# In the second layer's weight preparation, VectorE makes all low halves and GpSimd only the sums

## The chip, the cores and the metric

The kernel runs on one core of a Trainium2 chip. The time is the device time of one execution in microseconds (us), as the median of three timed runs. A profile of one further execution shows what each engine did: TensorE (PE in the rows, its weight loads PEld), VectorE (DVE), ScalarE (ACT), GpSimd (POOL) and SyncE (SP), which issues most DMAs.

## The reference

Attention with hash buckets gives `x` (1536 tokens x 512), and two dense layers follow. Only the second of them is touched here:

```
def _moe2_ref(x, w_in, w_out):        # x 1536x512, w_in 512x2048, w_out 2048x512
    h = x @ w_in
    g = h - np.tanh(h)
    return (g @ w_out).astype(np.float32)
```

The weights arrive as 64-bit words and are turned into 32-bit floats. A product in full precision is made of three TensorE products: each operand is split into a high half (the operand rounded to the format that TensorE multiplies fast) and a low half (the operand less its high half), and high*high, high*low and low*high are added up.

## The kernel before

After the attention and the first layer, `second_layer` works in two blocks (`sb` 0 and 1) of 768 tokens. Each block walks through 8 units `u`; a unit takes 256 of the 2048 hidden columns, so there are 16 units. In a unit, `h` is made by a scheme with seven instead of eight block products: the four blocks of the weights are combined into sums (`s1` to `s4`), the four blocks of the tokens into others (`t1` to `t4`, made once per block in `tokens`), and each of the seven products (`product`, L1084 to L1086, six matrix multiplications of 384 columns) goes into one of four PSUM banks. There are six PSUM slots `pt`; four of them hold results of the block through all units, so two are left for these banks, and TensorE can begin a further bank only when VectorE has read out an earlier one. These readings are `plus` (VectorE, `pl<-pt,ph` and `ph<-pt,ph` in the rows: bank plus an earlier partial sum) and, for one bank, `act`. In `act`, ScalarE makes `tanh` (L1097), VectorE subtracts (`pl<-pl,f` or `pl<-pt,f`), ScalarE rounds the result (L1099, `gh`), VectorE makes its low half (`gl<-pl,gh`). `outer2` (L1135) multiplies these by `w_out` and adds to the block's results.

`unit_weights` prepares a unit's weights. A DMA brings two tiles, `win` and `wout`, of 128 x 1024 floats. GpSimd makes four sums of 128x256 (`f<-wi`, `f<-f,wi`, `f<-wi,f`). Then four operand tiles and the two halves of `wout` are split: ScalarE writes the high half (L1056, L1061), another engine the low half by one subtraction. Before the change GpSimd makes four of these six low halves (all 128x512), and VectorE two (one 128x512, one 128x256). `tokens(1)`, the preparation of the second block's tokens, runs beside units of the first block, well ahead of use: GpSimd makes 16 sums and differences of 128x384 in the three buffers `t` (`t<-xh,xl`, `t<-t`), ScalarE rounds (L1002), VectorE makes eight low halves (`xl<-t,xh`, `t2l`, `t3l`, `t4l`).

All additions and subtractions go through one helper, so VectorE's and GpSimd's have one line, L890; the tiles in a row tell them apart. The order in which each engine gets its instructions is not the code's. Each operation is given to a planner (`op(engine, cost, key, ...)`) with a cost in us and a due time (`key`); `Plan.order` plays all engines forward by these costs and issues the operations in the order in which they start there. Every engine then works through its own list strictly in that order. The constants that this touches are `STEP = 1.06` (one product of a unit on TensorE) and the costs in `unit_weights`.

Of the kernel before, what the change touches and what calls it, by code (L numbers as in the profile page):

```python
# [123 lines left out]
class Plan:  # L124
# [11 lines left out]
    def buf(self, pool, tag, shape, dtype=F32):  # L136
        return Buf(self, pool, tag, shape, dtype)

    def op(self, eng, cost, key, fn, reads=(), writes=(), after=(), release=0.0, lat=None):
        o = Op()  # L140
        o.lat = self.LAT.get(eng, LATE) if lat is None else lat
        o.n, o.eng, o.cost, o.key, o.fn = len(self.ops), eng, cost, key, fn
        o.deps, o.users, o.bufs = {}, [], []
        for tok in reads:
            w = self.writer.get(tok)
            if w is not None:
                o.deps[w] = True
            self.readers.setdefault(tok, []).append(o)
        for tok in writes:
            w = self.writer.get(tok)  # L150
            if w is not None:
                o.deps[w] = True
            for r in self.readers.pop(tok, ()):
                if r is not o:
                    o.deps[r] = True
            self.writer[tok] = o
        for a in after:
            o.deps.setdefault(a, False)
        for tok in (*reads, *writes):
            b = tok[0] if isinstance(tok, tuple) else tok  # L160
            if isinstance(b, Buf) and b not in o.bufs:
                o.bufs.append(b)
                b.refs += 1
                self.by_pool.setdefault(b.pool, []).append(o)
        o.wait, o.ready = len(o.deps), release
        for d in o.deps:
            d.users.append(o)
        self.ops.append(o)
        return o
# [75 lines left out]
def tile_lsh_attention_moe(  # L245
# [13 lines left out]
    nc = tc.nc  # L259
# [18 lines left out]
    op, buf, room = plan.op, plan.buf, plan.room  # L278
# [65 lines left out]
    def dma(nbytes, key, out, in_, reads=(), writes=(), release=0.0):  # L344

        op("DMA", max(0.55, nbytes / 180e3), key, lambda: nc.sync.dma_start(out=out(), in_=in_()), reads, writes, release=release)
# [7 lines left out]
    def at(tick):  # L354
        return T_ATT + tick * TICK
# [324 lines left out]
    for g in range(len(pairs)):  # L680
# [7 lines left out]
        for n, (nm, half) in enumerate((("k", 0), ("q", 0), ("k", 1), ("q", 1))):  # L688
            key = k0 + PIECE * n * TICK if g else FIRST[n]
# [199 lines left out]
    def add(eng, out, in0, in1, sub=False):  # L889
        eng.tensor_tensor(out=out, in0=in0, in1=in1, op=ALU.subtract if sub else ALU.add)  # L890

    def unit_at(n):
        return moe_at(NBLK * KF) + n * UNIT
# [49 lines left out]
    def early(i, dtype=F32R):  # L943
        tag, pool = EARLY[i]
        return part2(pool, tag, dtype)
# [73 lines left out]
    def small(tag_pool):  # L1019
        pool, tag = tag_pool  # L1020
        return buf(pool, tag, [P, XB], F32)

    def unit_weights(sb, u):
        n = sb * NU + u
        odd = n % 2
        key = unit_at(n) - JIT - (UNIT0 if n < 2 else 0.0)
        gate = ["wd"] if odd else []
        w32 = [early(6 + 2 * odd + i, F32) for i in range(2)]
        for part in range(2):
            d = dram[u, part]  # L1030
            dma(
                P * DM * 8, unit_at(n) - FETCH + 3 * part, w32[part], lambda d=d: d.rearrange("p (m f) -> p m f", m=2),
                [("dram", u, part, i) for i in range(2)], [w32[part]], release=unit_at(n) - FETCH - 10.0,
            )
        win, wout = w32
        q = HB // 3 * 2

        def blk(i, j):
            return lambda: win()[:, i - 1, (j - 1) * q:j * q]

        sa, sb_ = (small(("f", "f")) for _ in range(2))
        lo_, up = slice(0, q), slice(q, 2 * q)
        op("POOL", 0.7, key, lambda: add(nc.gpsimd, sa()[:, up], blk(2, 1)(), blk(2, 2)()), [win], [(sa, 1)])
        op("POOL", 0.7, key + 0.1, lambda: add(nc.gpsimd, sa()[:, lo_], sa()[:, up], blk(1, 1)(), True), [win, (sa, 1)], [(sa, 0)])
        op("POOL", 0.7, key + 0.2, lambda: add(nc.gpsimd, sb_()[:, up], blk(1, 1)(), blk(2, 1)(), True), [win], [(sb_, 1)])
        op("POOL", 0.7, key + 0.3, lambda: add(nc.gpsimd, sb_()[:, lo_], blk(1, 2)(), sa()[:, lo_], True), [win, (sa, 0)], [(sb_, 0)])
        if odd:
            tiles = [buf("a2", f"a2{i}", [P, 2, DM], F32R) for i in range(4)]
        else:
            tiles = [early(10 + i) for i in range(4)]  # L1050
        srcs = (lambda: win()[:, 0], lambda: sa(), lambda: sb_(), lambda: win()[:, 1, q:])
        reads = ([win], [(sa, 0), (sa, 1)], [(sb_, 0), (sb_, 1)], [win])
        for i, (tl, src, rd) in enumerate(zip(tiles, srcs, reads)):
            w = DM if i < 3 else q
            eng, cost, e = (("POOL", 1.4, nc.gpsimd), ("DVE", 1.0, nc.vector))[i % 2]
            op("ACT", 0.02 + w * 0.00097, key + 0.5 + i, lambda tl=tl, src=src, w=w: nc.scalar.copy(tl()[:, 0, :w], src()), [*rd, *gate], [(tl, 0)], lat=0.4)  # L1056
            op(eng, cost * w / DM, key + 0.6 + i, lambda tl=tl, src=src, w=w, e=e: add(e, tl()[:, 1, :w], src(), tl()[:, 0, :w], True), [*rd, (tl, 0)], [(tl, 1)], lat=0.4)
        outs = []
        for i in range(2):
            tl = buf("raw", "raw", [P, 2, DM], F32R) if odd else early(14 + i)  # L1060
            op("ACT", 0.52, key + 5 + 2 * i, lambda tl=tl, i=i: nc.scalar.copy(tl()[:, 0], wout()[:, i]), [wout], [(tl, 0)], lat=0.4)  # L1061
            op("POOL", 1.4, key + 5.1 + 2 * i, lambda tl=tl, i=i: add(nc.gpsimd, tl()[:, 1], wout()[:, i], tl()[:, 0], True), [wout, (tl, 0)], [(tl, 1)], lat=0.4)
            outs.append(tl)
        at_ = {"a11": (0, 0), "a12": (0, q), "s2": (1, 0), "s1": (1, q), "s4": (2, 0), "s3": (2, q), "a22": (3, 0)}
        return {k: (tiles[i], o) for k, (i, o) in at_.items()}, outs
# [3 lines left out]
    def unit(sb, u, ops):  # L1069

        n = sb * NU + u
        key = unit_at(n)
        A, outs = unit_weights(sb, u)
        gs = [[buf("g2", x, [P, 2, HB], F32R) for x in ("gh", "gl")] for _ in range(2)]

# [103 lines left out]
    for m in range(KF):  # L1179
        for part, w in enumerate((w_in1, w_out1)):  # L1180
            if m < N_PRE:
                key = at(n_items - TICKS + C0) + (m + part / 2) * (TICKS - C0) * TICK / N_PRE
            else:
                key = T_MOE + (m - N_PRE + part / 2) * MTICK
# [85 lines left out]
```

## Time and profile before

| | us |
|---|---|
| median of three timed runs (775.41 to 777.13) | 775.73 |
| the profiled execution | 777.77 |
| its span, first to last instruction | 776.0 |
| second layer in it, about | 503 to 776 |
| block 1's tokens are prepared, about | 566 to 608 |
| first product of block 1, about | 638 |

The profiled execution is 2.04 us (0.26%) longer than the median; 1.77 us of it lie outside the span. In the second layer TensorE is the engine that hardly ever rests: from 500 to 776 us it stands still seven times, 7.3 us in all, before its last instruction.

### The profile page before, as it was taken

How to read it: one execution, taken by the hardware profiler on the slowest of the kernel's cores; microseconds unless marked ns; L12 is line 12 of the kernel's file. 1: busy time of each engine (PE TensorE's matmuls, PEld its weight loads, DVE VectorE, ACT ScalarE, POOL GpSimd, SP SyncE). 2: the span in 40 equal slices, each digit the busy share in tenths (PEclk: the TensorE clock that was granted, in tenths of full speed). 3: DMA queues.
4: the chain of work that ended last, by engine and by line, in shares of the span. 5: the costliest groups of instructions: out<-in, count | busy, mean ns of one | idle time of the engine just before them, and what ended most of it. 6: DMA issues, size and time to landing. Idle time of an engine off the chain costs nothing.

```text
span 776.0 us, 11414 instructions
## 1 busy us (share of the span) xinstructions
PE 755.0 (97%) x3901; PEld 655.8 (85%) x3901; DVE 562.5 (72%) x978; ACT 460.7 (59%) x926; POOL 400.8 (52%) x410
## 2 busy tenths in 40 slices
PE   7999999999999999999999999999998899999997
PEld 5999999999987888878887888888887798889885
DVE  6899899899998988754443566468689677667643
ACT  6999898998888556543333344365445355455422
POOL 5677668668545000022222386668599665656410
PEclk9999999999999999999999999999999999999999
DMA  6664656546690800035555417631111124111002
GB/s 171 166 154 117 139 131 141 138 106 145 164 394 3 344 37 0 28 95 174 165 160 166 146 58 225 210 115 62 56 55 54 55 67 175 58 55 57 26 1 82
DMA packets 32231, 91.05 MB, mean 117 GB/s; under 512 B 4518, under 2 KB 5414, under 8 KB 32172
## 3 DMA queue, kind: packets, MB, share of 16 engines
q1 hardware_dynamic: 31596, 89.69, 39.2%
q8 instruction: 31, 0.51, 0.3%
q10 hardware_dynamic: 576, 0.62, 0.2%
q14 instruction: 28, 0.23, 0.1%
HBM read 59.87 MB, written 11.53 MB: 92 GB/s over the span
## 4 chain that ended last, share of the span: by engine, by line
PE 82%; DVE 6%; ACT 3%; DMA 3%; POOL 2%; issue 2%; SPq 1%; ACTq 0%; POOLq 0%
PE pt L1135 10%; PE s L851 8%; PE pt L851 8%; PE pt L597 7%; PE pt L817 5%; PE pt L815 5%; PE pt L816 5%; PE s L1135 4%; PE pt L1084 4%; PE pt L1086 4%; PE pt L1085 4%; PE s L536 4%; PE s L537 4%; PE pt L575 4%; PE pt L576 4%
## 5 line engine op out<-in xcount | busy, mean ns | idle before, releaser
L932 POOL TENSOR_TENSOR t<-t,raw 128x512 uint32<-128x512 uint32 x32 | 45.1, 1409 | 163.0 <-ACT raw L927 114.0
L540 DVE TENSOR_SCALAR_CACHE_REDUCE p<-s 128x768 f32<-128x768 f32 x93 | 88.3, 950 | 14.5 <-PE s L537 13.7
L562 ACT ACTIVATE p<-p,mn 128x768 f32<-128x768 f32 x96 | 90.5, 943 | 10.2 <-DVE p L540 9.0
L597 PE MATMUL pt<-cst,p 128*128 128x128 f32 x576 | 90.9, 274 | 2.6 <-ACT p L562 1.6
L597 PEld LDWEIGHTS pt<-cst,p 128*128 128x128 f32 x576 | 71.9, 140 | 12.0 <-ACT p L562 2.3
L616 DVE TENSOR_TENSOR pl<-pt,ph 128x384 fp32r<-128x384 f32 x146 | 77.1, 547 | 2.0 <-ACT ph L613 1.7
L815 PE MATMUL pt<-xh,wi 128*128 128x512 f32 x192 | 75.6, 394 | 0.4 <-DVE u L666 0.4
L817 PE MATMUL pt<-xh,wi 128*128 128x512 f32 x192 | 75.5, 393 | 0.0
L816 PE MATMUL pt<-xl,wi 128*128 128x512 f32 x192 | 75.4, 393 | 0.0
L575 PE MATMUL pt<-ph,vt 128*128 128x384 f32 x192 | 74.9, 390 | 0.0
L834 DVE TENSOR_TENSOR pl<-f,ph 128x512 fp32r<-128x512 f32 x34 | 29.2, 859 | 60.9 <-ACT ph L831 60.9
L613 ACT CAST ph<-pt 128x384 fp32r<-128x384 f32 x146 | 68.3, 478 | 7.7 <-PE pt L575 4.3
L830 ACT ACTIVATE f<-pt 128x512 f32<-128x512 f32 x34 | 20.3, 598 | 86.6 <-PE pt L817 82.7
L536 PE MATMUL s<-b,a 128*128 128x384 f32 x186 | 66.6, 358 | 2.0 <-DVE p L540 1.9
L576 PE MATMUL pt<-pl,vt 128*128 128x384 f32 x192 | 65.1, 339 | 0.1
L537 PE MATMUL s<-d,c 77*128 77x384 f32 (+1 forms) x186 | 63.2, 340 | 0.0
L890 DVE TENSOR_TENSOR gl<-pl,gh 128x384 fp32r<-128x384 f32 x64 | 50.2, 787 | 16.0 <-ACT gh L1099 15.4
L851 PE MATMUL s<-ph,wo 128*128 128x512 f32 x192 | 60.2, 394 | 0.4 <-DVE xl L872 0.4
L851 PE MATMUL pt<-ph,wo 128*128 128x512 f32 x192 | 59.8, 392 | 0.0
L1099 ACT CAST gh<-pl 128x384 fp32r<-128x384 f32 x64 | 32.8, 514 | 44.9 <-DVE pl L890 44.7
L890 DVE TENSOR_TENSOR pl<-pl,f 128x384 f32<-128x384 f32 x48 | 43.8, 913 | 16.0 <-ACT f L1097 16.0
L609 POOL TENSOR_TENSOR pl<-f,ph 128x384 fp32r<-128x384 f32 x46 | 49.2, 1070 | 3.2
(258 smaller groups left out, 2101.1 us busy)
## 6 DMA issues: line engine op xcount, KB each, us to landing
wi<-in_moe_w_in_dram SPq DMA_DIRECT2D x16, 512.0 KB
wo<-in_moe_w_out_dram SPq DMA_DIRECT2D x16, 512.0 KB
raw<-in_moe_w_in_dram SPq DMA_DIRECT2D x16, 512.0 KB
raw<-in_moe_w_out_dram SPq DMA_DIRECT2D x16, 512.0 KB
w<-t SPq DMA_DIRECT2D x32, 256.0 KB
wi<-w SPq DMA_DIRECT2D x16, 512.0 KB
wo<-w SPq DMA_DIRECT2D x16, 512.0 KB
b<-kh SPq DMA_DIRECT2D x30, 192.0 KB
```

The costliest lines, as they stand in the source:

```text
L536: nc.tensor.matmul(o, a()[:, tok], b_()[:, kc], start=True, stop=False)
L537: nc.tensor.matmul(o, c_()[used, tok], d_()[used, kc], start=False, stop=True)
L562: lambda: nc.scalar.activation(out=p(), in_=p(), func=AF.Exp, bias=mn(), scale=-1.0, accum_out=sm()[:, h, t:t + 1],),
L575: nc.tensor.matmul(o()[:, :HB], vt()[:, c, :], ph()[:, :HB], start=(c == 0), stop=False)
L576: nc.tensor.matmul(o()[:, :HB], vt()[:, c, :], pl()[:, :HB], start=False, stop=(c == NT - 1))
L597: nc.tensor.transpose(pt()[:, t * P:(t + 1) * P], pc[:, c * P:(c + 1) * P], ident)
L815: nc.tensor.matmul(h(), w()[:, 0, c], xh[kk][:, cols], start=(kk == 0), stop=False)
L816: nc.tensor.matmul(h(), w()[:, 0, c], xl[kk][:, cols], start=False, stop=False)
L817: nc.tensor.matmul(h(), w()[:, 1, c], xh[kk][:, cols], start=False, stop=(kk == KD - 1))
L851: nc.tensor.matmul(o, x, y, start=st and i == 0, stop=sp and i == 2)
L890: eng.tensor_tensor(out=out, in0=in0, in1=in1, op=ALU.subtract if sub else ALU.add)
L1135: nc.tensor.matmul(o, x()[:, i, c], w()[:, y], start=m == 0 and k == 0, stop=m == KF - 1 and k == 2)
```

## The change

In `unit_weights` the low halves that GpSimd made (two of the four operand tiles, and both halves of `wout`) are given to VectorE, and the planner's cost for all VectorE low halves of 128x512 becomes 0.65 (it was 1.0 on VectorE and 1.4 on GpSimd). GpSimd keeps the four sums of each unit, the token sums and the earlier fetch work.

```diff
             w = DM if i < 3 else q
-            eng, cost, e = (("POOL", 1.4, nc.gpsimd), ("DVE", 1.0, nc.vector))[i % 2]
+            eng, cost, e = ("DVE", 0.65, nc.vector)
             op("ACT", 0.02 + w * 0.00097, key + 0.5 + i, lambda tl=tl, src=src, w=w: nc.scalar.copy(tl()[:, 0, :w], src()), [*rd, *gate], [(tl, 0)], lat=0.4)
             op(eng, cost * w / DM, key + 0.6 + i, lambda tl=tl, src=src, w=w, e=e: add(e, tl()[:, 1, :w], src(), tl()[:, 0, :w], True), [*rd, (tl, 0)], [(tl, 1)], lat=0.4)
...
-            op("POOL", 1.4, key + 5.1 + 2 * i, lambda tl=tl, i=i: add(nc.gpsimd, tl()[:, 1], wout()[:, i], tl()[:, 0], True), [wout, (tl, 0)], [(tl, 1)], lat=0.4)
+            op("DVE", 0.65, key + 5.1 + 2 * i, lambda tl=tl, i=i: add(nc.vector, tl()[:, 1], wout()[:, i], tl()[:, 0], True), [wout, (tl, 0)], [(tl, 1)], lat=0.4)
```

Since the costs steer the planner, the order of all engines in the second layer changes with it. In the rows below a name with a number is one tile; `a`, `wi`, `wo` and `raw` are operand tiles of weights, a row `x<-y,x 128x512` or `128x256` is a low half of weights.

VectorE at the beginning of the second layer, before: from a `plus` of the first unit to the `act` (`pl<-pt,f`) that frees its first bank, and the first layer's last low halves (L872).

```order
L890 TENSOR_TENSOR pl<-pt,ph 128x384
L890 TENSOR_TENSOR a_6247<-f,a_6247 128x512
L890 TENSOR_TENSOR a_6258<-wi_6083,a_6258 128x256
L890 TENSOR_TENSOR pl<-pt,f_6267 128x384
L872 TENSOR_TENSOR xl_123<-pt,xh_119 128x512
```

The same place now:

```order
L890 TENSOR_TENSOR pl<-pt,ph 128x384
L890 TENSOR_TENSOR wi_6221<-wi_6176,wi_6221 128x512
L890 TENSOR_TENSOR a_6244<-wi_6083,a_6244 128x512
L890 TENSOR_TENSOR a_6247<-f,a_6247 128x512
L890 TENSOR_TENSOR a_6256<-f,a_6256 128x512
L890 TENSOR_TENSOR a_6258<-wi_6083,a_6258 128x256
L890 TENSOR_TENSOR pl<-pt,f_6267 128x384
L872 TENSOR_TENSOR xl_123<-pt,xh_119 128x512
```

Three low halves of 128x512 have come in ahead of the `act`.

VectorE while block 1's tokens are prepared, between `plus` of the fifth unit of block 0 (the weights are those of the seventh), before:

```order
L890 TENSOR_TENSOR pl<-pt,ph 128x384 x2
L890 TENSOR_TENSOR pl<-pl,f_6935 128x384
L890 TENSOR_TENSOR wo_6946<-wi_6761,wo_6946 128x256
L890 TENSOR_TENSOR pl<-pl,f_6950 128x384
L890 TENSOR_TENSOR gl<-pl,gh 128x384
L890 TENSOR_TENSOR ph<-pt,ph 128x384
```

The same place now:

```order
L890 TENSOR_TENSOR pl<-pt,ph 128x384
L890 TENSOR_TENSOR wi_6917<-f,wi_6917 128x512
L890 TENSOR_TENSOR pl<-pl,f_6925 128x384
L890 TENSOR_TENSOR raw<-wo_6642,raw 128x512
L890 TENSOR_TENSOR pl<-pt,ph 128x384
L890 TENSOR_TENSOR gl<-pl,gh 128x384
L890 TENSOR_TENSOR wo_6947<-wi_6759,wo_6947 128x256
L890 TENSOR_TENSOR pl<-pl,f_6958 128x384
L890 TENSOR_TENSOR ph<-pt,ph 128x384
```

Two low halves of 128x512 and a subtraction of `act` now stand between the first `plus` and the second, which followed it directly.

GpSimd at that place, as a piece of the difference (rows with - were there before, rows with + are there now); `t` are the token sums of block 1:

```order
 L890 TENSOR_TENSOR t<-xh_119,xl_123 128x384
-L890 TENSOR_TENSOR raw<-wo_6648,raw 128x512
-L890 TENSOR_TENSOR t<-t 128x384
-L890 TENSOR_TENSOR f<-wi_6761 128x256
-L890 TENSOR_TENSOR f<-wi_6761,f 128x256
-L890 TENSOR_TENSOR wi_6818<-wi_6761,wi_6818 128x512
-L890 TENSOR_TENSOR wi_6920<-f,wi_6920 128x512
-L890 TENSOR_TENSOR raw<-wo_6648,raw 128x512
-L890 TENSOR_TENSOR f<-wi_6932 128x256
+L890 TENSOR_TENSOR f<-wi_6759,f 128x256
+L890 TENSOR_TENSOR t<-t 128x384
+L890 TENSOR_TENSOR f<-wi_6935 128x256
```

The four low halves have left; between two token sums only one or two weight sums are left in the list.

## Rows read from the trace of the kernel before

**Rows 1.** The page's first part: busy us, share of the span, instructions.
```profile
PE 755.0 (97%) x3901; PEld 655.8 (85%) x3901; DVE 562.5 (72%) x978; ACT 460.7 (59%) x926; POOL 400.8 (52%) x410
```

**Rows 2.** Stretches: length; busy us of PE, PEld, DVE, ACT, POOL; granted clock; DMA.
```profile
569.20:591.90 22.70, 19.73 (x97) 17.08 (x96) 19.75 (x24) 10.71 (x22) 22.62 (x20) 1.00 0.21 70
591.90:608.45 16.55, 13.86 (x67) 11.52 (x65) 15.56 (x17) 7.98 (x17) 15.96 (x14) 1.00 0.19 63
609.00:613.00 4.00, 3.95 (x12) 3.55 (x13) 2.44 (x4) 1.14 (x2) 2.35 (x3) 0.57 0.02 4
655.80:687.10 31.30, 31.30 (x158) 28.16 (x157) 22.34 (x32) 15.53 (x31) 20.62 (x18) 1.00 0.23 74
```

**Rows 3.** What TensorE waited for, 490 to 776 us: us in total, times, longest.
```profile
PE pt L1084 <- DVE ph L890: 4.2, 2, 3.1
PE pt L1084 <- DVE pl L890: 2.3, 3, 1.9
...
PE pt L1135 <- DVE pl L890: 0.3, 1, 0.3
```

**Rows 4.** TensorE in order of time: start, us, instruction, idle before it and its releaser.
```profile
519.36 0.44 PE L1084 MATMUL pt<-xh,a 128*128 128x384 f32 x1 [0.57 <-ACT ph L1106]
...
582.69 0.44 PE L1084 MATMUL pt<-xh,a 128*128 128x384 f32 x1 [1.90 <-DVE pl L890]
...
589.24 0.44 PE L1084 MATMUL pt<-xh,a 128*128 128x384 f32 x1 [1.07 <-DVE ph L890]
...
609.05 0.56 PE L1084 MATMUL pt<-xh,wo 128*128 128x384 f32 x1 [3.10 <-DVE ph L890]
```

**Rows 5.** VectorE's instructions by form, 569.2 to 609 us: count, busy us, mean ns.
```profile
L890 DVE TENSOR_TENSOR gl<-pl,gh 128x384 fp32r<-128x384 f32 x9 | 9.7, 1086 | 0.6 <-ACT gh L1099 0.6
L890 DVE TENSOR_TENSOR pl<-pl,f 128x384 f32<-128x384 f32 x6 | 7.5, 1254 | 1.6 <-ACT f L1097 1.6
L890 DVE TENSOR_TENSOR pl<-pt,ph 128x384 f32<-128x384 f32 x6 | 3.2, 544 | 0.0
```

**Rows 6.** GpSimd's instructions by form in the same stretch.
```profile
L890 POOL TENSOR_TENSOR t<-t 128x384 f32<-128x384 f32 x8 | 9.8, 1228 | 0.1
...
L890 POOL TENSOR_TENSOR f<-wi 128x256 f32<-128x256 f32 x6 | 5.8, 972 | 0.0
L890 POOL TENSOR_TENSOR raw<-wo,raw 128x512 fp32r<-128x512 f32 x2 | 3.2, 1612 | 0.0
...
L890 POOL TENSOR_TENSOR wi<-f,wi 128x512 fp32r<-128x512 f32 x1 | 1.3, 1298 | 0.0
```

**Rows 7.** VectorE in order of time, two instructions while GpSimd rests.
```profile
560.85 0.56 DVE L890 TENSOR_TENSOR pl<-pl,f 128x384 f32<-128x384 f32 x1 [0.65 <-ACT f L1097]
...
611.96 0.69 DVE L890 TENSOR_TENSOR wo<-f,wo 128x512 fp32r<-128x512 f32 x1 [0.15 <-ACT wo L1056]
```

**Rows 8.** VectorE in order of time, just ahead of the longest wait.
```profile
603.33 1.64 DVE L890 TENSOR_TENSOR pl<-pl,f 128x384 f32<-128x384 f32 x1
604.89 1.65 DVE L890 TENSOR_TENSOR t4l<-t,t4h 128x384 fp32r<-128x384 f32 x1
606.46 2.07 DVE L890 TENSOR_TENSOR gl<-pl,gh 128x384 fp32r<-128x384 f32 x2
608.45 0.55 DVE L890 TENSOR_TENSOR ph<-pt,ph 128x384 f32<-128x384 f32 x1
```

**Rows 9.** GpSimd in order of time, beside the rows of group 8.
```profile
603.08 1.47 POOL L890 TENSOR_TENSOR a<-wi,a 128x512 fp32r<-128x512 f32 x1
604.52 1.60 POOL L890 TENSOR_TENSOR a<-f,a 128x512 fp32r<-128x512 f32 x1
```

**Rows 10.** VectorE at the beginning of the second layer.
```profile
514.35 0.74 DVE L890 TENSOR_TENSOR a<-f,a 128x512 fp32r<-128x512 f32 x1
515.06 1.46 DVE L890 TENSOR_TENSOR a<-wi,a 128x256 fp32r<-128x256 f32 x1
516.87 0.56 DVE L890 TENSOR_TENSOR pl<-pt,f 128x384 f32<-128x384 f32 x1 [0.34 <-ACT f L1097]
```

## The prediction

> **What bounds it now.** I read the page's busy shares first, then TensorE's waits in the second layer, then each wait in the order of time, and last what VectorE and GpSimd did there. TensorE is busy 97% of the span, GpSimd 52%, VectorE 72% [rows 1]; as an average this says only that a gain must come out of TensorE's few gaps. In a stretch of two ordinary units TensorE is busy 31.30 of 31.30 us, VectorE 22.34 and GpSimd 20.62 [rows 2]: there nobody waits for either, and freeing GpSimd is worth nothing. From 490 us on TensorE waits 7.3 us: 4.2 for `plus`, 2.3 and 0.3 for VectorE's other work [rows 3], and 0.57 for ScalarE [rows 4]. The large waits stand together: 1.90, 1.07 and 3.10 us [rows 4], with one of 0.2 between them (what is left of the 2.3 and 4.2). That makes 6.3 us, all between 580 and 609 us, where `tokens(1)` is at work. There GpSimd is busy 38.58 of 39.25 us and VectorE 35.31 [rows 2]. After the 3.10 us wait, TensorE's granted clock over the next 4 us is 0.57, which is mostly its lower level, 1.2 GHz [rows 2]: 4 us at 0.57 do the work of 2.3, so 1.7 us more are lost. Behind the other two waits the clock stayed at 1.00 [rows 2, 4]. What can be won there is 6.3 + 1.7 = 8.0 us.
>
> Why is VectorE late? With GpSimd at rest, a 128x384 subtraction with both operands in SBUF takes 0.56 us and one of 128x512 takes 0.69 [rows 7]. In the token stretch the first kind takes 1.09 (`gl`) and 1.25 (`act`), while a `plus`, with an operand in PSUM, stays at 0.54 [rows 5]. Just ahead of the longest wait each VectorE subtraction lasts as long as the GpSimd instruction beside it: 1.64 and 1.65 beside 1.47 and 1.60 [rows 8, 9]. So the two engines hold each other up when VectorE reads both operands from SBUF; a VectorE instruction loses some 0.5 to 0.7 us, and a GpSimd one of 128x512 grows from 1.30 to 1.61 [rows 6].
>
> **The change part by part.** Four subtractions of 1.3 to 1.6 us per unit leave GpSimd, 64 in all, and come to VectorE at 0.69 each if nothing is in their way.
>
> *Token stretch, 569 to 608 us.* By count over the stretch, VectorE has 28 instructions with both operands in SBUF (9 `gl`, 6 `act` [rows 5], 8 token halves, 5 weight halves) and 13 `plus` and the like. The delay per such instruction is 0.53 (1.09 less 0.56) to 0.69 (1.25 less 0.56), say 0.57, so 16 us of VectorE's time is delay. The change brings 8 more at 0.69: +5.5 us. From GpSimd go 8 at about 1.5 us, 12 of its 38.6 us. In the new list its first token sums no longer stand behind low halves that wait for ScalarE; I expect 6 of the 16 token sums (1.23 us each [rows 6]) to slip ahead of the stretch, some 7 us. GpSimd is then busy 20 to 26 of 39 us instead of all of it, 51 to 68%. What is left to be waited for is shorter: weight sums at 0.97 and token sums at 1.23 instead of halves at 1.5 [rows 6], by which I lower the delay from 0.57 to 0.47. So 36 instructions x 0.47 x (0.51 to 0.68) = 8.6 to 11.5 us of delay in place of 16. VectorE's sum changes by 5.5 - 7.4 = -1.9 to 5.5 - 4.5 = +1.0 us: about nothing. But its 3.9 us of idle time in the stretch (39.25 less 35.31) is largely waiting for ScalarE instructions that themselves wait for GpSimd's late sums; up to 2.9 of it can go. Together VectorE gets through the stretch between 1.0 us later and 4.8 us earlier; I take the middle of 0 and 4.8, 2.4 us. If the longest wait shrinks to about 1.5 us, the clock should hold as it did behind 1.90 and 1.07 [rows 4]: another 1.7. Sum here: **-4.1 us**, bounds +1.0 and -8.0.
>
> *Beginning of the layer, 514 to 520 us.* Three low halves come ahead of the `act` that frees the first bank. Between the `plus` and this `act` lie now 2.5 us (514.35 to 516.87), with two low halves of 0.74 and 1.46 and 0.34 us of idle [rows 10]. With four of 0.69, and the narrow one between 0.69 and 1.46 (the delay by GpSimd included), it is 3.4 to 4.2 us: 0.9 to 1.7 later. TensorE already waits here, 0.2 for this `act` and 0.57 for a ScalarE copy behind it [rows 3, 4]; part of the delay runs into the second wait. I take **+0.8**, bounds 0 and +1.7.
>
> *Ordinary units.* In two units eight more low halves cost VectorE 5.5 us, and eight fewer GpSimd instructions save it up to 8 x 0.47 = 3.8: it goes from 22.34 to 24 or 26 of 31.30 us [rows 2]. That is room, but the lists are strict: a 0.69 us half, and sometimes two, now stands between two `plus`. The planner moved a piece of the outer products between two products for it, so I take **+0.3** over all such units, bounds 0 and +4.
>
> *GpSimd's list, DMAs, ScalarE.* GpSimd's sums come earlier; the weight tiles' DMAs now wait for VectorE's halves instead of GpSimd's, and a unit's weights are fetched more than one unit ahead, so a microsecond there is hidden by TensorE's 15.6 us per unit (half of 31.30). If that cover went, a late `win` would stop ScalarE, and then `tanh` and TensorE. Nothing is counted.
>
> Sum: -4.1 + 0.8 + 0.3 = **-3.0 us**. For the profiled execution that is 777.77 - 3.0 = 774.8; it lies 2.04 above the median of the timed runs, and I take the same 3.0 off the median: 775.73 - 3.0 = **772.7 us**.
>
> **The rivals.**
>
> *Nothing gained: VectorE takes GpSimd's place.* The sum above left VectorE's own load in the token stretch between -1.9 and +1.0. If the 3.9 us of idle stay, being waits for ScalarE and TensorE itself, VectorE is exactly as late as now, the longest wait stays and the clock falls again: 775.73 + 0 to 1.1, about **776**. For it speaks that VectorE is busy 35.31 of 39.25 us there [rows 2]; against it, that GpSimd is busier still and its list was the later one. The Trainium skill (Perfetto Trace Analysis, "Optimizing Scalar/DVE Operations") warns that moving work between GpSimd and VectorE might not help, as they share an SBUF read port; by it the end stays at 776, and the doubled durations agree that something is shared.
>
> *Full relief.* Where the two engines take turns, as just ahead of the longest wait [rows 8, 9], a moved half frees 1.30 us and takes 0.69: 0.6 us of the shared time, times 8, is 4.9 us, and with the 2.9 us of idle all 6.3 us and the clock's 1.7 are won: 775.73 - 8.0 + 0.8 = **768.5**. Against it: `plus` and waiting for ScalarE take VectorE's time too. The Trainium skill (SBUF — State Buffer, "SBUF: two separate sides") calls the shared pair of ports an exclusive lock, held for the whole instruction, whose loser is fully blocked; by it this rival would come true, and the paired durations agree, though no run here shows the lock itself.
>
> *Slower: halves in front of `plus`.* In ordinary units TensorE never waits today. A `plus` that finds a half of 0.69 us, or of 1.2 with GpSimd's delay, in front of it frees its bank that much later; TensorE has one product of 1.06 us, the planner's own price, to do before it needs the bank. From a delay of 1.06 us on it stands still. With 0.4 us in each of some 11 units, 4.4 us are lost, and with 0.8 at the beginning and a token stretch that gains only 1.5, the end is 775.73 + 3.7 = **779.4**.
>
> **How the numbers follow.** A measurement of this kernel can tell about 0.2%, 1.55 us, from no change. I give my forecast (some 770 to 774) 0.40, full relief 0.15, nothing gained 0.25, slower 0.20. Faster by over 0.2% (under 774.2): 0.40 + 0.15 = 0.55; within: 0.25; slower (over 777.3): 0.20. The range reaches to full relief below, and above a little into the slower case, leaving about 0.07 below and 0.13 above: 768.0 to 778.0. The forecast's own range is 770 to 774.2.
>
> **What would show it.** In the new profile GpSimd's busy time should fall by some 64 x 1.4 = 90 us and its 128x512 low halves be gone; VectorE's `gl` and `act` in the token stretch should fall from 1.1 to 1.25 us to 0.8 to 1.0; TensorE's waits of 1.90, 1.07 and 3.10 us should shrink to 4 us in all, without a granted clock near 0.57 behind them; the waits at 517 to 520 us should grow by about 0.8. I am wrong if the token stretch keeps 6 us of waits (VectorE as late as before), or if TensorE's waits show up in units after 620 us, where there are none today, most likely behind `plus`.

## The result, and the profile after

The changed kernel takes 768.76 us (median of four runs, 768.63 to 769.61) against 775.84 for the kernel before: a ratio of 0.9905, 95% interval 0.989 to 0.992. That is 7.1 us less, where 3.0 were forecast. It is faster, as forecast, and inside the range, but by more than twice the amount; the rival "full relief" with its 768.5 came nearest.

The first part of the new page answers to [rows 1]:

```profile
PE 752.3 (98%) x3901; PEld 654.2 (85%) x3901; DVE 579.0 (76%) x1042; ACT 461.0 (60%) x926; POOL 311.4 (41%) x346
```

GpSimd is busy 89.4 us less and VectorE only 16.5 us more. What TensorE waits for after 490 us (answering to [rows 3]; us in total, times, longest):

```profile
PE pt L1084 <- DVE pl L890: 2.3, 3, 1.1
PE pt L1135 <- DVE pl L890: 0.2, 1, 0.2
```

Of 7.3 us of waits 2.5 are left, and none is for `plus` into `ph` or for ScalarE. The same stretches as in [rows 2], with the same columns:

```profile
569.20:591.90 22.70, 21.46 (x105) 18.50 (x104) 20.69 (x29) 11.62 (x24) 14.63 (x13) 1.00 0.19 64
591.90:608.45 16.55, 16.55 (x85) 14.79 (x84) 14.57 (x25) 8.83 (x19) 7.21 (x7) 1.00 0.19 65
609.00:613.00 4.00, 4.00 (x21) 3.50 (x20) 2.44 (x5) 2.25 (x5) 0.00 (x0) 1.00 0.00 0
...
655.80:687.10 31.30, 31.30 (x158) 28.19 (x157) 22.81 (x39) 15.49 (x30) 7.62 (x8) 1.00 0.21 68
```

The clock stays at 1.00. In an ordinary stretch VectorE does seven instructions more and is busy only 22.81 us, 0.5 more than before. TensorE's instructions in order of time, around the longest wait that is left in the token stretch:

```profile
582.11 0.63 PE L1135 MATMUL s<-wi,gh 128*128 128x512 f32 x2
582.58 0.39 PE L1135 MATMUL s<-wi,gl 128*128 128x512 f32 x1
584.01 0.44 PE L1084 MATMUL pt<-wi,a 128*128 128x384 f32 x1 [1.04 <-DVE pl L890]
584.28 0.34 PE L1085 MATMUL pt<-wo,a 128*128 128x384 f32 x1
584.46 0.34 PE L1086 MATMUL pt<-wi,a 128*128 128x384 f32 x1
584.63 0.34 PE L1084 MATMUL pt<-wi,a 128*128 128x384 f32 x1
```

**A better measure of the loss.** In a row of matmuls without waits the starts lie 0.17 us apart for 128x384 and 0.23 for 128x512. Around this wait they lie 1.43 and 0.27 apart, in all 1.29 us more than usual, though the idle time is given as 1.04. So the text below counts what TensorE loses by the starts: the distance beyond 0.174 and 0.233 us, single places under 0.12 left out. A wait costs up to 0.27 us more than its idle time, and a low clock is counted too. The waits of before, 6.3 us of idle time and 1.7 for the clock in the prediction, are 9.1 us by this measure, the clock 1.5 of them. It closes: TensorE's last instruction ends 7.44 us earlier (763.10 for 770.54), the losses from 503 us on fall from 11.0 to 3.7 us. The rest of the 9.3 us by which the profiled spans differ lies behind TensorE's last instruction (5.5 us in the one, 3.6 in the other); the medians are not 9 but 7.1 apart.

### The profile page after: what moved, and what is told of

It is laid out like the page before. It is cut to its first block, busy times and chain, and to the rows that moved or that the text cites. A ratio compares the mean times of both kernels' runs of the same rounds, so it can differ in the third digit from the quotient of the medians.

```text
span 766.7 us, 11409 instructions
## 1 busy us (share of the span) xinstructions
PE 752.3 (98%) x3901; PEld 654.2 (85%) x3901; DVE 579.0 (76%) x1042; ACT 461.0 (60%) x926; POOL 311.4 (41%) x346
## 4 chain that ended last, share of the span: by engine, by line
PE 87%; DVE 7%; DMA 3%; ACT 2%; issue 1%; SPq 1%; ACTq 0%; DVEq 0%
PE pt L1135 11%; PE s L851 9%; PE pt L851 8%; PE pt L597 7%; PE pt L817 5%; PE pt L816 5%; PE pt L815 5%; PE s L1135 5%; PE pt L1084 5%; PE pt L1086 5%; PE pt L1085 5%; PE s L536 4%; PE pt L575 4%; PE s L537 4%; PE pt L576 4%
## 5 line engine op out<-in xcount | busy, mean ns | idle before, releaser
L890 POOL TENSOR_TENSOR f<-wi 128x256 f32<-128x256 f32 x32 | 30.0, 941 | 123.1 <-DVE a L890 34.2
L890 DVE TENSOR_TENSOR gl<-pl,gh 128x384 fp32r<-128x384 f32 x64 | 41.0, 642 | 9.0 <-ACT gh L1099 8.1
```

## The experiments

All kernels in one table. "Lost" is TensorE's loss in the profiled execution, by the starts; "stretch" is from 565 to 615 us, "later" from 615 us on; each entry is good to some 0.3 us. The kernel before had medians of 775.70 to 776.24 in the six sessions.

| kernel | us | ratio to before (95%) | lost 515 to 535 | 535 to 565 | stretch | later |
|---|---|---|---|---|---|---|
| before | 775.84 | 1 | 1.9 | 0 | 9.1 | 0 |
| the change | 768.76 | 0.9905 (0.989 to 0.992) | 1.9 | 0 | 1.8 | 0 |
| engine_only | 776.27 | 1.0011 (1.0001 to 1.0021) | 3.1 | 1.3 | 4.7 | 2.2 |
| order_only | 778.85 | 1.0043 (1.0031 to 1.0056) | 2.8 | 0 | 11.3 | 0 |
| dummy_read | 773.33 | 0.9975 (0.9965 to 0.9985) | 4.0 | 0 | 4.2 | 0.8 |
| dummy_write | 766.84 | 0.9889 (0.9876 to 0.9903) | 1.7 | 0 | 0.8 | 0 |
| dummy_write3 | 769.85 | 0.9922 (0.9905 to 0.9938) | 2.2 | 0 | 3.3 | 0 |
| dummy_none | 767.91 | 0.9902 (0.9887 to 0.9916) | 1.8 | 0 | 1.6 | 0 |
| cost_1 | 770.11 | 0.9930 (0.9915 to 0.9945) | 5.4 | 0 | 1.1 | 0 |
| units_5_7 | 774.55 | 0.9993 (0.9984 to 1.0002) | 2.0 | 0 | 6.8 | 0.3 |
| units_to_4 | 777.24 | 1.0019 (1.0010 to 1.0028) | 1.9 | 0 | 9.2 | 0 |
| units_to_7 | 769.09 | 0.9913 (0.9897 to 0.9929) | 1.9 | 0 | 1.7 | 0.3 |
| units_4_5 | 774.52 | 0.9981 (0.9969 to 0.9992) | 1.9 | 0 | 7.2 | 0 |
| units_4_7 | 771.65 | 0.9945 (0.9927 to 0.9962) | 2.0 | 0 | 3.0 | 0.3 |
| before_tok90 | 772.38 | 0.9957 (0.9945 to 0.9970) | 1.9 | 0 | 5.9 | 0 |
| after_tok90 | 770.54 | 0.9935 (0.9923 to 0.9948) | 1.9 | 0.6 | 2.8 | 0 |
| after_tok55 | 769.57 | 0.9922 (0.9905 to 0.9939) | 1.9 | 0 | 2.6 | 0 |
| before_spread | 772.36 | 0.9959 (0.9945 to 0.9973) | 1.9 | 0 | 5.2 | 0 |
| after_spread | 767.95 | 0.9906 (0.9892 to 0.9921) | 1.9 | 0 | 0.9 | 0 |
| none_early | 767.75 | 0.9898 (0.9881 to 0.9915) | 1.9 | 0 | 1.6 | 0 |

### Engine or order?

The change does two things: another engine executes, and the planner, with other costs, gives all engines other lists. Two kernels do one alone.

engine_only, against the kernel before:

```diff
-            eng, cost, e = (("POOL", 1.4, nc.gpsimd), ("DVE", 1.0, nc.vector))[i % 2]
+            eng, cost, e = (("POOL", 1.4, nc.vector), ("DVE", 1.0, nc.vector))[i % 2]
...
-            op("POOL", 1.4, key + 5.1 + 2 * i, lambda tl=tl, i=i: add(nc.gpsimd, ...
+            op("POOL", 1.4, key + 5.1 + 2 * i, lambda tl=tl, i=i: add(nc.vector, ...
```

> The four low halves run on VectorE, but the planner still counts them as GpSimd's at 1.4 us (and VectorE's own two at 1.0), so the lists of all engines are made by the old plan. Theory A (the two engines hold each other up over SBUF): GpSimd's busy time in the second layer falls as in the change, VectorE's `gl` and `act` between 569 and 609 us fall to 0.9 us or less, TensorE's waits from 580 to 610 us fall from 6.3 to 2 us or less; time 768 to 772. Theory B (the new costs give better lists): the old lists keep most of the old waits; time 774 to 777.

It took 776.27 us, in theory B's range: the relief over SBUF came, and no time was won. `gl` and `act` fell to 0.70 and 0.76 us in the token stretch, and the loss there to 4.7 us (one wait of 2.29 us, behind it a granted clock of 0.57). But 1.2 us more were lost at the beginning and 3.5 in units where TensorE had never waited. VectorE in order of time at such a place, ahead of a wait of TensorE of 0.64 us that ends at 537.30:

```profile
533.94 1.23 DVE L890 TENSOR_TENSOR wi<-wo,wi 128x512 fp32r<-128x512 f32 x1
535.09 1.09 DVE L890 TENSOR_TENSOR gl<-pl,gh 128x384 fp32r<-128x384 f32 x1
536.10 0.68 DVE L890 TENSOR_TENSOR wo<-wo,wo 128x512 fp32r<-128x512 f32 x1
536.70 0.55 DVE L890 TENSOR_TENSOR pl<-pt,ph 128x384 f32<-128x384 f32 x1
```

Two halves that the plan had counted on GpSimd stand in front of `plus`, without idle time: the rival "halves in front of `plus`" as the prediction told it, in the old lists.

order_only, against the changed kernel:

```diff
-            eng, cost, e = ("DVE", 0.65, nc.vector)
+            eng, cost, e = ("DVE", 0.65, (nc.gpsimd, nc.vector)[i % 2])
...
-            op("DVE", 0.65, key + 5.1 + 2 * i, lambda tl=tl, i=i: add(nc.vector, ...
+            op("DVE", 0.65, key + 5.1 + 2 * i, lambda tl=tl, i=i: add(nc.gpsimd, ...
```

> The planner's costs and lists are those of the change, but GpSimd still makes the four low halves. Theory A: GpSimd is busy nearly all of 569 to 609 us, VectorE's `gl` and `act` there stay at 1.1 to 1.25 us, TensorE's waits there are 5 us or more; time 774 to 779. Theory B: time 768 to 771.

It lost 11.3 us in the stretch (waits of 3.93 and 2.69 us) and took 778.85 us, the time that theory A gave. But theory A's reason is only a part of it: `act` took 1.18 us there, `gl` only 0.90, as in the change, and VectorE was busy only 26.91 of the 39.30 us from 569.2 us on. Ahead of the longest wait it stood idle for ScalarE, and ScalarE for a token sum of GpSimd, whose list the plan had made without the low halves:

```profile
583.04 0.99 POOL L890 TENSOR_TENSOR t<-t 128x384 f32<-128x384 f32 x1
...
584.05 0.51 ACT L1002 CAST t4h<-t 128x384 fp32r<-128x384 f32 x1 [3.02 <-POOL t L890]
...
584.60 0.56 DVE L890 TENSOR_TENSOR t4l<-t,t4h 128x384 fp32r<-128x384 f32 x1 [2.11 <-ACT t4h L1002]
```

So neither half of the change wins anything alone; together they win 7.1 us. In the old lists the halves on VectorE stand in front of `plus`; in the new ones GpSimd is late unless it is really relieved.

cost_1, the change with the planner's cost for VectorE's halves at 1.0:

```diff
-            eng, cost, e = ("DVE", 0.65, nc.vector)
+            eng, cost, e = ("DVE", 1.0, nc.vector)
...
-            op("DVE", 0.65, key + 5.1 + 2 * i, ...
+            op("DVE", 1.0, key + 5.1 + 2 * i, ...
```

> The whole change, but the planner counts VectorE's low halves at 1.0 us of 128x512 and not at 0.65: other lists with the same work on the same engines. If it is enough that the planner knows that VectorE does the halves: 767 to 770.5, without waits after 620 us. If the low cost of 0.65 is what makes good lists: 771 or more, with new waits behind `plus` in ordinary units as in engine_only.

770.11 us, within the first theory's bounds, and no waits after 620 us: that the planner knows where the halves run is enough there. It lost its time at the beginning of the layer, 5.4 us with a granted clock of 0.67 between 527 and 532 us. The token stretch lost only 1.1.

### What does VectorE lose to GpSimd?

Four kernels have the same lists on TensorE, VectorE and ScalarE. They are the change, with six dummies per unit planned on GpSimd that work on a tile that nobody reads any more in the second layer:

```diff
+        for k in (0.6, 0.6, 2.6, 5.1, 5.1, 7.1):
+            op("POOL", 0.95, key + k, lambda: add(nc.gpsimd, spare, spare, spare, True), release=key + k)
```

In dummy_write the call is one `nc.gpsimd.memset(spare, 0.0)`, in dummy_write3 three of them, in dummy_none nothing.

> The whole change, and beside it GpSimd makes six subtractions of 128x336 per unit on a spare tile that nobody reads (about 0.92 us each, 5.5 us per unit, as much as it was relieved of); the output is the same. Theory A (SBUF shared by the two engines): VectorE's `gl` and `act` rise again to 1.0 us or more in the token stretch, and as VectorE now has eight halves more there, the time is 775 to 785. Theory C (what counted was that GpSimd's own list was late, so that ScalarE and VectorE waited for its sums): the list is as long as before, so the time goes to 774 to 777, with VectorE's durations as in the change.

> As dummy_read, but each dummy is a memset of 128x336 on GpSimd, which reads nothing from SBUF (its duration is not known from any row; it is read from this run). Theory A, if what is shared is the reading of SBUF: VectorE's durations in the token stretch stay at 0.9 us or less, time 768 to 771; if writing alone blocks as well, `gl` and `act` rise in proportion to the memsets' time. Theory C: as late as dummy_read, in proportion to the memsets' time.

> Same lists once more; each dummy is now three memsets (3 x 0.378 us as dummy_write showed, against 0.98 for a dummy subtraction), so GpSimd's list is as long as in dummy_read and reads no more than in dummy_none. Theory A (VectorE and GpSimd hold each other up only where both read SBUF): VectorE's `gl` and `act` in the token stretch stay at 0.75 us or less, time 766.5 to 768.5. Theory C (GpSimd's own list is late): 772 to 775, as dummy_read's 773.3.

> The planner counts the six dummies of GpSimd per unit (0.95 us each) as in dummy_read and dummy_write, so TensorE, VectorE and ScalarE get the same lists as there, but nothing is issued for them: the whole change with lists planned for a GpSimd that is busier than it is. If dummy_write was faster than the change because of its lists: 766 to 767, as dummy_write or a little less. If the memsets themselves had any part in it: nearer to the change, 768 to 769.

The same stretch of the four engines' work, by the columns of [rows 2], in dummy_none, dummy_write3 and dummy_read:

```profile
505.00:763.00 258.00, 254.72 (x1260) 227.18 (x1258) 191.66 (x316) 128.02 (x253) 75.03 (x73) 1.00 0.19 67
```
```profile
505.00:763.00 258.00, 253.94 (x1256) 226.47 (x1256) 192.84 (x315) 127.64 (x252) 173.74 (x343) 1.00 0.19 65
```
```profile
505.00:763.00 258.00, 251.76 (x1240) 223.17 (x1239) 214.85 (x313) 125.23 (x249) 161.05 (x163) 1.00 0.18 63
```

With the memsets GpSimd is busy 98.7 us more than in dummy_none and VectorE 1.2 us; with the subtractions GpSimd 86.0 us and VectorE 23.2. VectorE's 96 instructions with an operand in PSUM (`pl<-pt,ph`, `ph<-pt,ph`, `pl<-pt,f`) take 0.55 us in dummy_none and in dummy_read alike. So it is GpSimd's reading of SBUF that VectorE pays for, where both its operands lie there, and not GpSimd's being busy: theory A, with the lists of the other engines held fixed. The Trainium skill (SBUF — State Buffer, "Who interferes with whom") says just this, that a VectorE instruction with two SBUF inputs collides with a GpSimd instruction that reads SBUF and not with one that only writes it; the trace agrees. In time, the reading costs 773.33 less 769.85, 3.5 us, and the longer list of GpSimd (theory C) 769.85 less 767.91, 1.9 us: dummy_write3 fell between the ranges of the two theories, and both are real. The size of the first was overrated: dummy_read came out under both ranges written for it, and its `gl` in the stretch rose to 0.85 us only. dummy_none (767.91) and dummy_write (766.84) cannot be told apart by their intervals.

### Which units?

Here the change, engine and cost, is made in some units only (`n` counts from 0):

```diff
+            moved = 5 <= n <= 7
+            eng, cost, e = ("DVE", 0.65, nc.vector) if moved else (("POOL", 1.4, nc.gpsimd), ("DVE", 1.0, nc.vector))[i % 2]
...
```

The halves of `wout` are switched in the same way. Theory D, which two of these texts name, is that VectorE is late by how much work of both engines falls into the same 39 us; before_tok90, further below, has it in full.

> Only the units whose low halves fall into the token stretch (the sixth to the eighth, n from 5 to 7) are changed, engine and cost; all others are as before. If the gain lies in the token stretch alone: TensorE's waits from 580 to 610 us fall from 6.3 to 1 to 2.5 us with no fall of the clock, the beginning of the layer stays as before; 767.5 to 770. If the halves moved in the other units are needed too (their sums come earlier, the lists have room): 771 to 775.

> The change in the first five units alone (n up to 4), none of whose moved halves falls into the token stretch. Theory D: the token sums begin at about 552 us, as in the change, and the waits of the token stretch fall by half or more; 770 to 773. Theory A alone: the token stretch keeps 6 us of waits; 775 to 777.

> The change in block 0's eight units (n up to 7), block 1 as before. In the second block TensorE never waits, before or after; so both theories: 768 to 770, as the whole change. If block 1 had a part in it: 771 or more.

units_to_7 gave 769.09, the whole gain: block 1 has no part in it. But neither half of block 0 does it. units_5_7 kept 6.8 us in the stretch although its `gl` and `act` were down to 0.91 and 0.83 us, much as in the change. Its longest wait is again 3.09 us, now at 587.43, and the clock fell behind it (0.58 over the next 4 us). Here it is a moved half that stands directly in front of `plus` on VectorE; beside GpSimd's token sums of 1.30 and 1.44 us it takes 1.48 us in place of 0.69:

```profile
585.43 1.48 DVE L890 TENSOR_TENSOR raw<-wo,raw 128x512 fp32r<-128x512 f32 x1
586.84 0.54 DVE L890 TENSOR_TENSOR pl<-pt,ph 128x384 f32<-128x384 f32 x1
...
587.43 0.69 PE L1086 MATMUL pt<-wi,a 128*128 128x384 f32 x1 [3.09 <-DVE pl L890]
```

units_to_4 kept 9.2, and its token sums did not begin at 552 us as expected but at 565: one half of the sixth unit stood ahead of them in GpSimd's list and waited 6.80 us for ScalarE. From this came theory E, that what the change frees is GpSimd's list, so that the sums begin at 551.6 and not at 566.4 us.

> The change in the fifth and sixth unit alone (n 4 and 5), whose four low halves on GpSimd stood ahead of the first token sum in the trace of before and waited there for ScalarE. The low halves of the seventh and eighth unit, which lie in the token stretch, stay on GpSimd. Theory E (the low halves block GpSimd's list: it idled 9.7 us behind ScalarE just before the token sums, and the change frees that list): the sums begin at about 552 us and the waits of the token stretch fall from 9.1 us to 5 or less; 770 to 773. Theory A alone: the halves that collide in the stretch are still there; 774.5 to 777.

> The whole change, but block 1's tokens are due 15 us later (TOK1 55), so that their sums begin at about 566 us as they did before, with GpSimd relieved of all its low halves. Theory E: the waits of the stretch come back in good part, 4 us or more with the clock's loss; 772 to 776. Theory A (relief over SBUF is what counts, the start of the sums not): 768 to 770.

> The change in the fifth to the eighth unit (n 4 to 7): the blocking low halves ahead of the token sums and those in the stretch, nothing else. Theory E with A: both are needed and these four units are all that counts; 768 to 770, against 774.55 with the sixth to the eighth alone. If the relief of the first units counts as well: 771 or more.

Theory E fell. In units_4_5 the sums began at 554.2 us and the stretch still lost 7.2. In after_tok55 (`TOK1 = 55.0` for 70.0 in the changed kernel) they began at 567.4, a microsecond later than before, and it lost 2.6. GpSimd in order of time in units_4_5, and VectorE beside it:

```profile
599.96 1.61 POOL L890 TENSOR_TENSOR wo<-wo,wo 128x512 fp32r<-128x512 f32 x1
601.52 1.47 POOL L890 TENSOR_TENSOR a<-wi,a 128x512 fp32r<-128x512 f32 x1
602.95 1.61 POOL L890 TENSOR_TENSOR a<-f,a 128x512 fp32r<-128x512 f32 x1
```
```profile
601.77 1.63 DVE L890 TENSOR_TENSOR pl<-pl,f 128x384 f32<-128x384 f32 x1
603.33 1.65 DVE L890 TENSOR_TENSOR t4l<-t,t4h 128x384 fp32r<-128x384 f32 x1
604.90 2.07 DVE L890 TENSOR_TENSOR gl<-pl,gh 128x384 fp32r<-128x384 f32 x2
606.89 0.54 DVE L890 TENSOR_TENSOR ph<-pt,ph 128x384 f32<-128x384 f32 x1
```

It is [rows 8, 9] once more, and behind it TensorE waited 3.09 us, as 3.10 before. Of the kernels in this section the two that leave the seventh and eighth unit's halves on GpSimd keep that wait (3.09, and 3.15 in units_to_4). Where they are moved, engine and list, there is none at this place. But these halves alone do not make it: before_tok90 below leaves them on GpSimd too, its token sums are over earlier, and there is no wait there. So the longest wait came from these halves and the token sums together. Of the two earlier ones, 1.90 and 1.07, units_4_7 has a wait of 2.74 left, and units_to_7, which moves four units more ahead of it, 0.19 and 1.00. What in those units makes that difference stays open.

### How much comes together?

> The kernel before, its low halves on GpSimd, with block 1's tokens due 20 us earlier in the plan (TOK1 90 for 70), so that their sums begin a unit sooner. Theory D (what makes VectorE late is how much work of both engines falls into the same 39 us, and the change helps largely because it lets the token sums begin 15 us earlier): the waits of TensorE between 575 and 612 us, their clock loss included, fall from 9.1 us to 5 or less; 769 to 773. Theory A alone (the low halves themselves on GpSimd): the same work meets over SBUF elsewhere, 774 to 777.

> The whole change, and block 1's tokens due 20 us earlier (TOK1 90). Theory D: the last waits of the token stretch (0.20 and 1.04 us, with what a wait costs besides, 1.75 in all) shrink to 0.5 or less; 767 to 768. If the sums now meet the beginning of the layer: 769 to 771.

> The kernel before, all its low halves on GpSimd; only the plan of block 1's token preparation is spread: it is due 18 us earlier (TOK1 88) and its two batches of eight sums stand 36 us apart and not 20. Theory F (a wait of TensorE comes where GpSimd is full for over 10 to 20 us without a break, so that VectorE's delays add up): the 40 us without a break, 565 to 605 us, fall into two pieces, the waits of the stretch (9.1 us with the clock's loss) go to 3 to 5; 769.5 to 772.5. Theory A without it (the same instructions meet, so the same delay): 774 to 777.

> The same spread in the changed kernel. Theory F: GpSimd is never full for over 10 us, the 1.75 us that are left of the token stretch go to 0.5 or less, 767 to 768. If the earlier first batch finds VectorE too busy with the halves of ordinary units, as after_tok90 did at 567 and 570 us: 769.5 to 771.

before_spread moves no work between engines:

```diff
-TOK1 = 70.0
+TOK1 = 88.0
...
-            key = base + 20.0 * k
+            key = base + (20.0 + 16.0 * sb) * k
```

GpSimd's busy time (the fifth after the length) in pieces of 10 us, in the kernel before and then in before_spread:

```profile
555.00:565.00 10.00, 10.00 (x50) 8.75 (x49) 5.03 (x8) 4.02 (x7) 3.85 (x5) 1.00 0.06 25
565.00:575.00 10.00, 10.00 (x53) 9.16 (x52) 8.87 (x12) 5.09 (x11) 9.92 (x9) 1.00 0.32 105
575.00:585.00 10.00, 8.10 (x42) 7.15 (x41) 8.73 (x10) 5.32 (x12) 9.92 (x9) 1.00 0.01 2
585.00:595.00 10.00, 8.93 (x44) 7.51 (x43) 9.08 (x10) 3.99 (x8) 9.48 (x9) 1.00 0.31 105
595.00:605.00 10.00, 9.80 (x49) 8.38 (x48) 9.35 (x12) 5.54 (x12) 9.92 (x9) 1.00 0.08 28
```
```profile
555.00:565.00 10.00, 10.00 (x49) 8.72 (x48) 9.42 (x11) 4.03 (x8) 9.92 (x10) 1.00 0.16 53
565.00:575.00 10.00, 7.60 (x40) 6.60 (x39) 8.65 (x12) 5.29 (x11) 9.07 (x8) 1.00 0.30 105
575.00:585.00 10.00, 10.00 (x51) 8.88 (x49) 5.88 (x9) 4.46 (x9) 4.82 (x5) 1.00 0.01 2
585.00:595.00 10.00, 10.00 (x51) 8.95 (x51) 8.11 (x11) 5.07 (x12) 10.00 (x10) 1.00 0.30 105
595.00:605.00 10.00, 8.48 (x43) 7.42 (x42) 9.89 (x12) 5.16 (x11) 9.92 (x8) 1.00 0.00 0
```

With one rest for GpSimd in the middle, VectorE catches up (5.88), the loss falls from 9.1 to 5.2 us (3 to 5 were expected), and the kernel takes 772.36 us: half of the change's gain, without the change. before_tok90, which only begins earlier, won as much (772.38), though its 5.9 us of loss are above theory D's 5. In the changed kernel a plain shift loses: after_tok90 took 770.54 and not 767 to 768, with waits at 567 us, behind a `gl` of 1.38 us, and at 570 us, behind an ordinary unit's half of 1.20 us, both in front of `plus`. With the spread it lost 0.9 us in the stretch where the change lost 1.8, but 767.95 us cannot be told from the change's time. Theory F holds in its direction, not as a rule on length: in units_4_5 GpSimd was full for only 12 us (11.92 of 595 to 607) and the 3.09 us wait came all the same.

### A better version?

> A try for a better version: dummy_none (GpSimd planned busier than it is) with the weights of the first two units prepared 6 us earlier (UNIT0 6). The waits at the beginning of the layer, 1.83 us in dummy_none, are for VectorE's low halves ahead of `act`; if they go: 766 to 767. If the earlier halves only collide with the end of the first layer: 768 to 769.

`UNIT0` (6.0 for 0.0) on dummy_none took 767.75 us, and the beginning of the layer still lost 1.9. The lowest median is dummy_write's 766.84. All its four runs (766.57 to 767.11) lie below the change's four, but the intervals of the two ratios overlap (0.9876 to 0.9903, 0.989 to 0.992), so no version is shown to beat the change.

## Why the prediction was right in direction and too small

**Token stretch, -4.1: -7.4 by the starts.** This is the step that failed, and in it the term for VectorE's time, "-1.9 to +1.0, about nothing": its busy time fell by 4.5 us. Both kernels do the same TensorE work, 162 matmuls, in these two stretches, the first of before:

```profile
569.20:609.05 39.85, 33.59 (x162) 28.60 (x161) 35.91 (x42) 18.69 (x39) 39.18 (x33) 1.00 0.20 66
```
```profile
569.20:603.30 34.10, 32.86 (x162) 28.64 (x161) 31.44 (x46) 18.75 (x40) 21.09 (x19) 1.00 0.19 60
```

The stretch became 5.75 us shorter, where I had taken 2.4 and 4.8 at most. VectorE's busy time fell from 35.91 to 31.44 us, its idle time only by 1.3 (3.94 to 2.66), where up to 2.9 was to come from it: the gain came from the delays, and the idle time was the small part. Three of its forms in the new stretch, with the delays that are left:

```profile
L890 DVE TENSOR_TENSOR gl<-pl,gh 128x384 fp32r<-128x384 f32 x7 | 6.3, 895 | 0.1
L890 DVE TENSOR_TENSOR pl<-pl,f 128x384 f32<-128x384 f32 x6 | 5.2, 875 | 1.3 <-ACT f L1097 1.3
...
L890 DVE TENSOR_TENSOR raw<-wo,raw 128x512 fp32r<-128x512 f32 x2 | 2.5, 1226 | 0.0
```

Summed over all forms against 0.56, 0.69 and 0.42 us (a narrow half at its shortest) the delay falls from 16.8 to 8.5 us; I had 16 and 8.6 to 11.5, and took it as if the middle were sure. A further 2 us of VectorE's work (two `gl`, a `plus`, a narrow half) now fall outside. GpSimd's share, 62%, lay in my 51 to 68%. Six of the 16 token sums do stand ahead of the stretch, as I wrote, but two stood there before (566.38 us), so four slipped ahead, 5 us and not 7. The rest of the 7.4 is the clock, which came back as forecast, with 1.5 us by the starts for my 1.7. What a wait costs beyond its idle time, 0.27 us, I had not known; it is inside the 5.75.

**Beginning, +0.8: 0.** The halves did come ahead of `act`, and it begins 0.6 us later:

```profile
516.60 0.96 DVE L890 TENSOR_TENSOR a<-wi,a 128x256 fp32r<-128x256 f32 x1
517.49 0.55 DVE L890 TENSOR_TENSOR pl<-pt,f 128x384 f32<-128x384 f32 x1
```

TensorE waits 1.08 us for it, in place of 0.20, but the wait of 0.57 for ScalarE is gone, and the loss by the starts is 1.3 us as before. The lower bound was right.

**Ordinary units, +0.3: 0.** No wait after 585 us. VectorE's load grew by 0.5 us in two units and not by 2 to 4, while GpSimd's busy time there went from 20.62 to 7.62 us. engine_only shows that this rested on the new lists: in the old ones the "slower" rival loses 4.7 us outside the stretch.

**The rivals.** "Nothing gained" was ruled out: VectorE's delays were halved. "Full relief" had the time nearly right, in part by luck: its 4.9 us for taking turns lies near the 4.5 us by which VectorE's busy time fell, but about 2 us of these are work that now falls outside the stretch, its 2.9 us of idle time were 1.3, and it counted 0.8 us lost at the beginning, where nothing was. The Trainium skill's warning (Perfetto Trace Analysis, "Optimizing Scalar/DVE Operations") that such a move may not help did not hold for the change. engine_only won nothing either, but not because of the shared read port that the page names: its `gl` and `act` became shorter, and the time went into waits behind the moved halves.

## What to carry to other kernels

When work moves between engines under a planner, test the move and the new order apart: here neither alone won anything and both together won 7 us. Where two engines hold each other up, work taken from one can shorten the other's instructions as well: here VectorE had eight wide halves more in the stretch and was busy 4.5 us less, though 2 of these are work that fell outside. Look for such a gain in the busy time of the engine that is late, not only in its idle time. A pile of work can be cut by its due times too; spreading the token sums alone gave half of the gain.

## What the runs showed of the hardware

**A wait costs TensorE more than its idle time**, by 0.23 to 0.27 us, as in the rows around the longest wait that is left in the profile after: the last matmul ahead and the first behind each lie further from their neighbour.

**The clock does not follow the length of a wait.** The 4 us behind a wait of 2.08 us in before_tok90, of 2.74 in units_4_7 and of 3.15 in units_to_4, in this order:

```profile
584.60:588.60 4.00, 4.00 (x14) 4.00 (x15) 3.72 (x4) 2.25 (x6) 4.00 (x4) 0.57 0.00 0
```
```profile
585.40:589.40 4.00, 3.96 (x21) 3.66 (x22) 3.89 (x5) 1.54 (x4) 2.54 (x3) 1.00 0.63 224
```
```profile
610.90:614.90 4.00, 4.00 (x19) 3.54 (x20) 2.25 (x4) 1.76 (x3) 2.28 (x3) 1.00 0.02 4
```

The shortest of the three was followed by the lower level, 1.2 GHz for most of the 4 us, the two longer ones by 2.4 GHz throughout. The prediction's "about 1.5 us, then the clock should hold" came true, but it was no rule: in cost_1 the clock held behind a wait of 1.79 us at 518 us and fell behind two of 0.55 and 0.97 us at 526 and 528 us.
